# Loading the first tile as two halves on two queues, and half of the key weights on a third, at the head of a two-layer linear-attention and MLP kernel

## The chip, the cores and the metric

The kernel runs on one core of a Trainium2 chip. The metric is the device time of one execution in microseconds (us). Before the change it is 323.23 us, the median of three runs (323.01 to 323.62).

The engines are named as the profile names them: PE (TensorE, matrix multiplications; PEld its weight loads), DVE (VectorE), ACT (ScalarE), POOL (GpSimd) and SP (SyncE, which here only issues DMAs). A letter q behind an engine's name (SPq, ACTq, POOLq) means its instruction queue, for instance when it issues a DMA.

## What is computed

x has 2048 tokens of 512 features in bf16. Two blocks, A and B, are applied in turn, twice over, each with a residual:

```python
def _A_ref(x, wqkv, wo):            # linear attention, 32 heads of 16
    q, k, v = heads of (x @ wqkv)
    phi = lambda t: jnp.where(t > 0, t + 1, jnp.exp(t)) + 1e-6
    pq, pk = phi(q), phi(k)
    kv = jnp.einsum("bhsd,bhse->bhde", pk, v)
    z = jnp.einsum("bhsd->bhd", pk)
    o = einsum(pq, kv) / (einsum(pq, z)[..., None] + 1e-6)
    return merged(o) @ wo

def _B_ref(x, w1, b1, w2, b2):      # MLP, 512 -> 1792 -> 512
    y = _layernorm(x, axis=-1)
    h = _gelu(jnp.einsum("bsd,df->bsf", y, w1) + b1)
    return jnp.einsum("bsf,fd->bsd", h, w2) + b2

x = x + _A_ref(_layernorm(x), A_wqkv, A_wo)
x = x + _B_ref(_layernorm(x), B_w1, B_b1, B_w2, B_b2)
x = x + _A_ref(_layernorm(x), A_wqkv, A_wo)
x = x + _B_ref(_layernorm(x), B_w1, B_b1, B_w2, B_b2)
```

## The kernel before

**Tiling.** The tokens are 16 tiles of 128 (numbered 0 to 15), in four chunks of four tiles: chunk c is rows 512c to 512c+511, and partition p of it holds four neighbouring rows, one for each tile. Everything stays in on-chip memory between the blocks; the inputs are read once and the result is written once.

**An order written out by hand.** The kernel first builds a graph of named operations (`G.op`), each with its engine, what it reads and what it writes. `CONF["ORDER"]` lists for every engine the names in the order in which they are issued, and `CONF["PLACES"]` says which buffer slot each tile takes. `Settled.run` (line 144) takes both as they stand; nothing is chosen while the program runs. An engine waits at an instruction until everything that this one reads is there, and all that is listed behind it on that engine waits too. `assign_waits` (line 186) turns the dependencies into semaphore waits.

**The loads at the start.** `CONF["LOADS"]` (line 243) lists them: name, issuing queue, what, and behind which earlier operation. SP issues `x0` (tile 0, 128 KB), `x1` (tiles 1 to 3, 384 KB), `wka` and `wkc` (quarters 0 and 1 of the key weights, 128 KB each), then `xc1` (chunk 1, 512 KB), which waits until `x0` has landed, then `wq` (512 KB, query weights), `xc3`, and, behind the first two DMA transposes, `xc2`. ACT issues `wkb` (quarter 2), held until the constant `onesm` is written, and `wkd` (quarter 3). A quarter d is rows 128d to 128d+127 of the 512x512 key weights, the contraction slice of one matmul.

**The head, tile by tile.** While the loads are under way PE runs warm-up matmuls on a constant (`warm0`, seven of 512 columns, and `warm1` to `warm8`, of 256). For tile 0, DVE makes statistics (`statsA0_0`, line 775; `aggrA0_0`, line 777) and centres the tile (`cenA0_0`, line 789); PE transposes it (`PTC0`, line 825, four transposes); ACT copies the transposed tile out (`tcC0`, line 835). Then PE multiplies it with the four quarters of the key weights, in four separate operations `K0_0a` to `K0_0d` in the order that `ks0` gives ("2|0|3|1"). The division by the standard deviation, a power on POOL (`vepsA0_0`, line 782, `powA0_0`, line 784), follows as a scale on ACT (`expk0_0`, line 847, `reluk0_0`, line 858); DVE ends phi with `mink0_0` (line 860) and `phik0_0` (line 864). Tile 1 goes the same way (`cenA0_1`, `PTC1`, `tcC1`, `K0_1`, which needs all four quarters). Tiles 2 and 3 are normalised on DVE (`normA0_2`, `normA0_3`, line 803) before PE transposes them (`PTA0_2`, `PTA0_3`, copies `tcA0_2`, `tcA0_3`). The statistics of tile 3 are made on ACT (`sumA0_3`, line 766, stands ahead of `tcC0` in ACT's order). On DVE `statsA0_5`, which needs chunk 1, stands ahead of `normA0_3`. From tile 4 on the transposes are DMAs on SP (`TA0_n`, line 812).

With the key features `pk` of a tile, PE adds to the running product of normalised input and keys (`G0_n_0`, line 984). Query projections (`Q0_c_k`, lines 896 and 909) stand in between; the first, `Q0_0_*`, needs the transposes of all four tiles of chunk 0 and `wq`.

**POOL's order** starts with the small constants `id0`, `neghalf`, `bdm0`, `bdm1`, `id1` (lines 719 to 734: the identity for PE's transposes and the block-diagonal mask), and goes on with `vepsA0_0`, `powA0_0`, `negA0_3` and so on. Its own DMAs (`wv`, `wo`, `w1`, `w2`, line 728) come some 30 us later.

After the head come the attention's output (line 1123), the MLP (lines 1153 and 1190), and the second layer in the same manner.

Of the kernel before, what the change touches and what calls it, by code (L numbers as in the profile page):

```python
# [1359 lines left out]
```

## Time and profile before

| | |
|---|---|
| median of the runs | 323.23 us (323.01 to 323.62) |
| the profiled execution | 323.1 us, of which the profile's span is 321.9 us |
| PE busy in the span | 318.0 us (99%) |
| DVE, ACT, POOL busy | 218.1, 189.3, 145.5 us (68%, 59%, 45%) |
| read from and written to memory | 8.00 and 2.10 MB |
| granted TensorE clock, mean | 1.00 |

In the views of the profile a row of the timeline is: start in us from the span's start, duration in us, engine, line of the kernel, operation, what is written and read, number of instructions merged in the row, and, in brackets, the idle time of the engine ahead of it with what ended it. A row of the DMA view is: destination, source, issuing queue, number of DMAs, size of each, and the median time in us from issue to landing. Consecutive matmuls overlap in the pipeline: four of 512 columns in a row show 1.03 us, and the next four start 0.86 us after them.

### The profile page before, as it was taken

To read this page: it belongs to the slowest core of one execution; us is meant where nothing else is said; L and a number is where in the kernel's file an instruction comes from. 1 tells how busy PE (TensorE), PEld (TensorE's weight loads), DVE (VectorE), ACT (ScalarE), POOL (GpSimd) and SP (SyncE) were. 2 spreads that over 40 slices of the span, in tenths; PEclk is the share of its full clock that TensorE was granted. 3 is DMA by queue.
4 is the path that set the end of the run, shared out by engine and by line. 5 is a ranking of instruction groups with operands and counts; after the bars stand their busy time and mean duration, and the time that the engine had idled before them with its cause. 6 is when DMAs were issued, how large, how long until landed. Compare 5 with 4: busy or idle time off the path is not lost.

```text
span 321.9 us, 4748 instructions
## 1 busy us (share of the span) xinstructions
PE 318.0 (99%) x1703; PEld 157.4 (49%) x1703; DVE 218.1 (68%) x529; ACT 189.3 (59%) x324; POOL 145.5 (45%) x216
## 2 busy tenths in 40 slices
PE   8999999999999999999999999999999999999997
PEld 3444554666444444444444444558544444444444
DVE  5998789999786774028848899999889881101103
ACT  5898656797730636667962367979634442663320
POOL 6573978688655355101822415887454163000000
...
DMA packets 52355, 21.68 MB, mean 67 GB/s; under 512 B 47532, under 2 KB 50860, under 8 KB 52332
## 3 DMA queue, kind: packets, MB, share of 16 engines
...
q10 hardware_dynamic: 432, 0.30, 0.3%
q8 instruction: 13, 0.21, 0.3%
q14 instruction: 10, 0.08, 0.1%
HBM read 8.00 MB, written 2.10 MB: 31 GB/s over the span
## 4 chain that ended last, share of the span: by engine, by line
PE 97%; DMA 2%; DVE 0%; issue 0%
PE ps L1153 30%; PE ps L1190 29%; PE ps L1123 9%; PE ps L879 8%; PE ps L896 6%; PE ps L984 4%; PE ps L1013 4%; DMA t<-in_A_x_dram 2%; PE ps L909 2%; PE ps L1176 1%; PE ps L970 1%; PE ps L1034 1%; PE ps L1057 1%; PE ps L1100 1%; DVE stats L775 0%; PE ps L1048 0%
## 5 line engine op out<-in xcount | busy, mean ns | idle before, releaser
L1158 ACT ACTIVATE gT<-ps,b1c 128x512 bf16<-128x512 f32 (+1 forms) x140 | 77.0, 601 | 68.7 <-PE ps L1153 68.1
L1153 PE MATMUL ps<-t,w 128*128 128x512 bf16 (+1 forms) x560 | 102.5, 336 | 0.0
L1190 PE MATMUL ps<-w,gT 128*128 128x512 bf16 x434 | 98.6, 379 | 0.0
L1153 PEld LDWEIGHTS ps<-t,w 128*128 128x128 bf16 x560 | 54.8, 98 | 43.7 <-ACT gT L1158 0.2
L1190 PEld LDWEIGHTS ps<-w,gT 128*128 128x128 bf16 x434 | 42.5, 98 | 50.4
L784 POOL TENSOR_TENSOR rstd<-veps,neghalf 128x1 f32<-128x1 f32 x64 | 39.0, 625 | 41.1 <-DVE veps L782 38.9
L847 ACT ACTIVATE eb<-ps 128x512 bf16<-128x512 f32 x62 | 35.4, 606 | 19.3 <-PE ps L896 7.3
L1200 DVE TENSOR_TENSOR yb<-ps,xsb 128x512 bf16<-128x512 f32 x15 | 10.2, 688 | 41.4 <-PE ps L1190 41.4
L775 DVE BATCH_NORM_STATS2 stats<-xsb 128x6 f32<-128x512 f32 x48 | 32.0, 681 | 0.3
L1123 PE MATMUL ps<-gtb,t 128*128 128x512 bf16 x128 | 31.4, 379 | 0.0
L879 PE MATMUL ps<-wqkv,t 128*128 128x512 bf16 x128 | 30.9, 379 | 0.3 <-ACT t L835 0.3
L858 ACT ACTIVATE rb<-ps 128x512 bf16<-128x512 f32 x43 | 25.3, 607 | 5.8 <-PE ps L879 5.8
L798 ACT ACTIVATE yb<-xsb,nmr,rstd 128x512 bf16<-128x512 f32 x21 | 16.9, 814 | 15.1 <-POOL nmr L795 15.1
L896 PE MATMUL ps<-wqkv,t 128*128 128x512 bf16 x96 | 24.1, 379 | 0.0
L1089 POOL TENSOR_TENSOR t<-t,rr 128x512 bf16<-128x512 bf16 x18 | 19.3, 1072 | 9.0 <-DVE rr L1085 6.4
L782 POOL TENSOR_SCALAR veps<-mv 128x1 f32<-128x1 f32 x35 | 8.2, 236 | 32.7 <-DVE mv L777 31.3
L1196 DVE TENSOR_TENSOR xsb<-ps,xsb 128x512 f32<-128x512 f32 x16 | 10.8, 678 | 17.9 <-PE ps L1190 17.9
L1139 POOL TENSOR_TENSOR xsb<-xsb,b2b 128x512 f32<-128x512 f32 x17 | 21.4, 1267 | 3.0 <-DVE yb L803 2.9
L1077 POOL TENSOR_TENSOR lr<-t,zrow 128x512 f32<-128x512 bf16 x14 | 16.5, 1179 | 7.3 <-ACT zrow L997 4.5
L1123 PEld LDWEIGHTS ps<-gtb,t 128*128 128x128 bf16 x128 | 12.5, 98 | 14.5
L803 DVE TENSOR_SCALAR yb<-xsb,mv,rstd 128x512 bf16<-128x512 f32 x27 | 14.5, 542 | 7.3 <-POOL rstd L784 6.0
L879 PEld LDWEIGHTS ps<-wqkv,t 128*128 128x128 bf16 x128 | 12.1, 98 | 14.7 <-ACT t L835 0.9
...
## 6 DMA issues: line engine op xcount, KB each, us to landing
...
out_dram<-yb SPq DMA_DIRECT2D x15, 128.0 KB, 2.0
t<-in_A_x_dram SPq DMA_DIRECT2D x3, 512.0 KB, 4.8
t<-yb SPq DMA_TRANSPOSE x62, 2.5
wqkv<-in_A_wqkv_dram SPq DMA_DIRECT2D x1, 512.0 KB, 5.9
wqkv<-in_A_wqkv_dram POOLq DMA_DIRECT2D x1, 512.0 KB, 4.7
wo<-in_A_wo_dram POOLq DMA_DIRECT2D x1, 512.0 KB, 5.3
t<-in_A_x_dram SPq DMA_DIRECT2D x1, 384.0 KB, 3.3
```

Source lines behind the costliest of these rows:

```text
L775: G.op("dve", lambda e: e.bn_stats(stats[:, s.slot, :], src()), 620, reads=src_keys, writes=[k + "s"], tiles=[s, *src_tiles], name=f"stats ...
L784: G.op("pool", lambda e: e.tensor_tensor(rstd[:, s.slot:s.slot + 1], veps[:, s.slot:s.slot + 1], neghalf[:], op=ALU.pow), 570, reads=[k + ...
L847: G.op("act", lambda e: e.activation(eb[:, et.slot, :], bank(bt), ACT.Exp, scale=by()), 478, reads=[src_key, *more_keys], writes=[f"e{tag} ...
L858: G.op("act", lambda e: e.activation(rb[:, rt.slot, :], bank(bt), ACT.Relu, scale=by()), 478, reads=[src_key, *more_keys], writes=[f"r{tag ...
L879: ins = e.matmul(bank(b), lhsT=yTa(yT)[:, dt, k * P:(k + 1) * P], rhs=wqkv[:, dt, D:2 * D], start=(i == 0 and n == 0), stop=(i == len(part ...
L896: ins = e.matmul(bank(b), lhsT=yTa(yT)[:, dt, k * P:(k + 1) * P], rhs=wqkv[:, dt, 0:D], start=(dt == 0), stop=(dt == DT - 1))
L1089: lambda e, d=d, tok=tok, heads=heads: e.tensor_tensor(heads(tok()), heads(tok()), rr[:, d.slot, :].unsqueeze(2).broadcast_to([P, H, DH]), ...
L1123: ins = e.matmul(bank(wb), lhsT=yTa(pq)[:, kt, k * P:(k + 1) * P], rhs=gtb[:, kt, :], start=(kt == 0), stop=(kt == DT - 1))
L1139: G.op("pool" if on_pool else "dve", lambda e: e.tensor_tensor(xsb[:, st, :], xsb[:, st, :], b2b[:], op=ALU.add), 1120 if on_pool else 600 ...
L1153: ins = e.matmul(bank(b, n), lhsT=w1[:, dt, ft * P:(ft + 1) * P], rhs=yTa(yT)[:, dt, k0 * P:k1 * P], start=(dt == 0), stop=(dt == DT - 1))
L1158: G.op("act", lambda e, ft=ft, b=b, k0=k0, k1=k1, n=n: e.activation(gT[:, g.slot, ft * 512 + k0 * P:ft * 512 + k1 * P], bank(b, n), ACT.Ge ...
L1190: ins = e.matmul(bank(b), lhsT=gT[:, g.slot, ft * 512 + k * P:ft * 512 + (k + 1) * P], rhs=w2[:, ft, :], start=(ft == 0), stop=(ft == FT - 1))
```

## The change

1. `x0` is cut in two DMAs of 64 partitions each: `x0a` first on SP's queue, `x0b` first on ACT's. `xc1` now waits for both.
2. Of the key weights, quarter 0 (`wkb`) is issued by ACT behind `x0b`, without the hold on `onesm`; quarter 1 (`wka`) by SP in the place of before; quarters 2 and 3 (`wkp`, one DMA of 256 KB) by POOL, behind `id1` and ahead of `vepsA0_0`. `wkc` and `wkd` are gone.
3. `ks0` becomes "0|1|23": `K0_0c` now holds the two matmuls of quarters 2 and 3, and `K0_0d` is gone.
4. The orders of all engines are listed anew for the head, up to about the first MLP matmuls; from there on they are the same name by name. `PLACES` changes with them. Two of the tiny operations `veps` move from DVE to POOL (`vepsA0_12`, `vepsB0_7`).
5. New code that this configuration does not use: chunk orders (`CHUNKS` is 0, 1, 2, 3 in all three stages, the order of before) and a mixed form of the denominator (`by_half`, which no chunk asks for).

```diff
-    LOADS=[['x0', 'sp', 'x', 0, 0, 1, ''], ['x1', 'sp', 'x', 0, 1, 4, ''],
-           ['wkb', 'act', 'wk', 0, 2, 3, 'ones'], ['wka', 'sp', 'wk', 0, 0, 1, ''],
-           ['wkd', 'act', 'wk', 0, 3, 4, ''], ['wkc', 'sp', 'wk', 0, 1, 2, ''],
-           ['xc1', 'sp', 'x', 1, 0, 4, 'x0'], ['wq', 'sp', 'wq', 0, 0, 4, ''], ...
+    LOADS=[['x0a', 'sp', 'half', 0, 0, 0, ''], ['x0b', 'act', 'half', 1, 0, 0, ''],
+           ['x1', 'sp', 'x', 0, 1, 4, ''], ['wkb', 'act', 'wk', 0, 0, 1, ''],
+           ['wka', 'sp', 'wk', 0, 1, 2, ''], ['wkp', 'pool', 'wk', 0, 2, 4, ''],
+           ['xc1', 'sp', 'x', 1, 0, 4, 'x0a x0b'], ['wq', 'sp', 'wq', 0, 0, 4, ''], ...
...
 "sp":
-  "x0 x1 wka wkc xc1 wq xc3 TA0_0 TA0_1 xc2 TA0_5 TA0_4 TA0_7 ...
+  "x0a x1 wka xc1 wq xc3 TA0_0 TA0_1 TA0_5 TA0_4 xc2 TA0_7 ...
 "pe":
-  "warm0 warm8 warm2 warm6 PTC0 warm1 warm7 warm5 warm4 warm3 K0_0a K0_0b PTC1 K0_0c K0_0d
-   PTA0_2 K0_1 PTA0_3 K0_2 K0_3 G0_0_0 G0_1_0 Q0_0_2 Q0_0_1 Q0_0_0 K0_5 G0_2_0 K0_4 ...
+  "warm0 warm7 warm4 warm5 warm8 PTC0 warm1 warm6 warm3 warm2 K0_0a K0_0b PTC1 K0_0c
+   PTA0_2 K0_1 PTA0_3 K0_2 G0_0_0 K0_3 G0_1_0 Q0_0_1 Q0_0_2 Q0_0_0 K0_5 G0_2_0 K0_4 ...
 "act":
-  "wkb wkd sumA0_3 tcC0 sqA0_3 tcC1 reluk0_0 tcA0_2 expk0_0 tcA0_3 expk0_1 reluk0_1 ...
+  "x0b wkb sumA0_3 tcC0 sqA0_3 tcC1 expk0_0 tcA0_2 reluk0_0 expk0_1 tcA0_3 reluk0_1 ...
 "dve":
-  "... normA0_2 statsA0_5 normA0_3 aggrA0_5 normA0_1 statsA0_4 mink0_0 aggrA0_4 phik0_0 ...
+  "... normA0_2 statsA0_5 normA0_3 normA0_1 mink0_0 aggrA0_5 phik0_0 statsA0_4 mink0_1 ...
 "pool":
-  "id0 neghalf bdm0 bdm1 id1 vepsA0_0 powA0_0 negA0_3 vepsA0_2 ...
+  "neghalf id0 bdm0 bdm1 id1 wkp vepsA0_0 powA0_0 negA0_3 vepsA0_2 ...
...
-        "ks0": "2|0|3|1"
+        "ks0": "0|1|23"
...
+        def load_half(name, queue, h, after):
+            G.parts[("x0", 0)] = (("x0", 0, 0), ("x0", 0, 1))
+            ps_ = slice(64 * h, 64 * h + 64)
+            loaded[name] = dma(queue, lambda e: e.dma_start(
+                t4[ps_, x0[0].slot, 0:D].rearrange("p (k d) -> p k d", k=1), rows(x_dram, 0)[ps_, 0:1, :]),
+                [("x0", 0, h)], [x0[0]], name=name, kb=64, after=after)
```

More of the change, by code (lines that the diff above doesn't have):

```diff
@@ L242 @@
     WARM=[[512, 512, 512, 512, 512, 512, 512], [256], [256], [256], [256], [256], [256], [256], [256]],
-    LOADS=[['x0', 'sp', 'x', 0, 0, 1, ''], ['x1', 'sp', 'x', 0, 1, 4, ''], ['wkb', 'act', 'wk', 0, 2, 3, 'ones'], ['wka', 'sp', 'wk', 0, 0, 1, ''], ['wkd', 'act', 'wk', 0, 3, 4, ''], ['wkc', 'sp', 'wk', 0, 1, 2, ''], ['xc1', 'sp', 'x', 1, 0, 4, 'x0'], ['wq', 'sp', 'wq', 0, 0, 4, ''], ['xc3', 'sp', 'x', 3, 0, 4, ''], ['xc2', 'sp', 'x', 2, 0, 4, '']],
+    LOADS=[['x0a', 'sp', 'half', 0, 0, 0, ''], ['x0b', 'act', 'half', 1, 0, 0, ''], ['x1', 'sp', 'x', 0, 1, 4, ''], ['wkb', 'act', 'wk', 0, 0, 1, ''], ['wka', 'sp', 'wk', 0, 1, 2, ''], ['wkp', 'pool', 'wk', 0, 2, 4, ''], ['xc1', 'sp', 'x', 1, 0, 4, 'x0a x0b'], ['wq', 'sp', 'wq', 0, 0, 4, ''], ['xc3', 'sp', 'x', 3, 0, 4, ''], ['xc2', 'sp', 'x', 2, 0, 4, '']],
+    CHUNKS=[[0, 1, 2, 3], [0, 1, 2, 3], [0, 1, 2, 3]],
     ORDER={
         "sp":
[1 row of a table removed]
[1 row of a table added]
             "TA0_11 b1 Tb1 TP0_1_3 b2 TP0_1_1 TP0_1_0 TP0_1_2 TB0_0 TB0_1 TB0_2 TB0_3 TB0_7 TP0_2_1 TB0_5 TB0_4 TB0_6 TP0_2_2 "
@@ L709, in load_w @@
                                [f"{which}_{d}" for d in range(d0, d1)], name=name, kb=128 * (d1 - d0), after=after)
+        def load_half(name, queue, h, after):
[4 more added lines that the diff above has]
+                [("x0", 0, h)], [x0[0]], name=name, kb=64, after=after)
         for name, queue, what, at, lo, hi, behind in cf["LOADS"]:
             after = [loaded[b] for b in behind.split()]
-            if what == "x":
+            if what == "half":
+                load_half(name, queue, at, after)
+            elif what == "x":
                 load_x(name, queue, at, lo, hi, after)
@@ L751, in build_kernel, with by_token, by_half @@
             G.op("pe", warm, sum(cols) / 1.2, tiles=[wu], name=f"warm{n}", n=len(cols))
-        def by_token(L, c):
-            return eng(f"den{L}_{c}") == "tok"
+        def by_token(L, c, k=0):
+            way = eng(f"den{L}_{c}")
+            return way == "tok" or (way == "half" and k >= 2)
+        def by_half(L, c):
+            return eng(f"den{L}_{c}") == "half"
+        tokq = {}
         def norm(src, src_keys, src_tiles, double, on_act, tag, src16=False, head=False, centred=None):
@@ L887, in attn_q, with fn @@
         def attn_q(L, c, yT, pq):
-            if by_token(L, c):
-                for k in range(4):
+            half = by_half(L, c)
+            own = pq
+            if half:
+                own = tokq[(L, c)] = Tile(T4, f"pqt{L}_{c}")
+            n = 2 * P if half else 4 * P
+            if not by_token(L, c):
+                for kt in range(DT):
+                    b = Tile(psum, f"q{L}_{c}_{kt}" + "c" * half, "q")
+                    def fn(e, kt=kt, b=b):
+                        for dt in range(DT):
+                            ins = e.matmul(bank(b, n), lhsT=wqkv[:, dt, kt * P:(kt + 1) * P], rhs=yTa(yT)[:, dt, 0:n],
+                                           start=(dt == 0), stop=(dt == DT - 1))
+                        return ins
+                    G.op("pe", fn, 4 * MM if n == D else 4 * (n / 2.4 + 2.5), reads=[f"yT{L}_{4 * c + k}" for k in range(n // P)] + ["wq"], writes=[f"q{L}_{c}_{kt}" + "c" * half],
+                         tiles=[b, yT], name=f"Q{L}_{c}_{kt}" + "c" * half, lat=MM_DRAIN, n=4)
+                    phi(b, f"q{L}_{c}_{kt}" + "c" * half, lambda kt=kt: yTa(pq)[:, kt, 0:n], f"pq{L}_{c}_{kt}" + "c" * half, [pq], f"q{L}_{c}_{kt}" + "c" * half, n=n)
+            for k in range(4):
+                if by_token(L, c, k):
                     b = Tile(psum, f"q{L}_{c}_{k}", "q")
@@ L900, in attn_q, with attn_z @@
                          tiles=[b, yT], name=f"Q{L}_{c}_{k}", lat=MM_DRAIN, n=4)
-                    phi(b, f"q{L}_{c}_{k}", lambda k=k: t4[:, pq.slot, k * D:(k + 1) * D], f"pq{L}_{c}_{k}", [pq],
+                    phi(b, f"q{L}_{c}_{k}", lambda k=k: t4[:, own.slot, k * D:(k + 1) * D], f"pq{L}_{c}_{k}", [own],
                         f"q{L}_{c}_{k}")
-                return
-            for kt in range(DT):
-                b = Tile(psum, f"q{L}_{c}_{kt}", "q")
-                def fn(e, kt=kt, b=b):
-                    for dt in range(DT):
-                        ins = e.matmul(bank(b), lhsT=wqkv[:, dt, kt * P:(kt + 1) * P], rhs=yTa(yT)[:, dt, :],
-                                       start=(dt == 0), stop=(dt == DT - 1))
-                    return ins
-                G.op("pe", fn, 4 * MM, reads=[f"yT{L}_{4 * c + k}" for k in range(4)] + ["wq"], writes=[f"q{L}_{c}_{kt}"],
-                     tiles=[b, yT], name=f"Q{L}_{c}_{kt}", lat=MM_DRAIN, n=4)
-                phi(b, f"q{L}_{c}_{kt}", lambda kt=kt: yTa(pq)[:, kt, :], f"pq{L}_{c}_{kt}", [pq], f"q{L}_{c}_{kt}")
         zfirst = {}
-        def attn_z(L, c, pks):
-            by_sum = [int(v) for v in (eng("zc0") or "").split()] if L == 0 else list(range(NC - 1))
+        def attn_z(L, c, pks, order):
+            by_sum = [int(v) for v in (eng("zc0") or "").split()] if L == 0 else order[:NC - 1]
+            others = [v for v in order if v not in by_sum]
             def fold(add):
@@ L973, in attn_z, with attn_g_held @@
             G.op("pe", fn, 400, reads=[f"pk{L}_{4 * c + k}" for k in range(4)] + ["onesm"], writes=[f"zc{L}_{c}"], tiles=[b, *pks], name=f"Z{L}_{c}", lat=MM_DRAIN, n=16)
-            total(b, f"zc{L}_{c}", f"zs{L}_{c}", bool(L) or c != min(v for v in range(NC) if v not in by_sum))
-            if L == 0 and by_sum and c == max(v for v in range(NC) if v not in by_sum):
+            total(b, f"zc{L}_{c}", f"zs{L}_{c}", bool(L) or c != others[0])
+            if L == 0 and by_sum and c == others[-1]:
                 fold(True)
-        def attn_g_held(L, st, k, y, ykey, pk, gb):
-            parts = [(dc,) for dc in range(DT)] if st == ST - 1 else [tuple(range(DT))]
+        def attn_g_held(L, st, k, y, ykey, pk, gb, first, last):
+            parts = [(dc,) for dc in range(DT)] if last else [tuple(range(DT))]
             for part in parts:
@@ L984, in fn @@
                         ins = e.matmul(ps[:, gb.slot + dc, :], lhsT=yb[:, y.slot, dc * P:(dc + 1) * P], rhs=pkb[:, pk.slot, :],
-                                       start=(st == 0), stop=(st == ST - 1))
+                                       start=first, stop=last)
                     return ins
                 keys = [f"g{L}_{dc}" for dc in part]
-                G.op("pe", fn, len(part) * MM, reads=[ykey, f"pk{L}_{st}"] + (keys if st else []), writes=keys,
+                G.op("pe", fn, len(part) * MM, reads=[ykey, f"pk{L}_{st}"] + ([] if first else keys), writes=keys,
                      tiles=[y, pk, gb], name=f"G{L}_{st}_{part[0]}", lat=MM_DRAIN, n=len(part))
@@ L1004, in attn_g_out, with attn_g_chunk @@
                 copy(gtb[:, dc, :], gb, f"g{L}_{dc}", ("gt", dc), dc % 2, f"g{L}_{dc}", off=dc)
-        def attn_g_chunk(L, c, ys, ykeys, pks):
+        def attn_g_chunk(L, c, ys, ykeys, pks, first, last):
             for dc in range(DT):
@@ L1017, in attn_g_chunk @@
                      tiles=[b, *ys, *pks], name=f"G{L}_{c}_{dc}", lat=MM_DRAIN, n=4)
-                if c == 0:
+                if first:
                     G.op("dve", lambda e, dc=dc, b=b: e.tensor_scalar(gacc[:, dc, :], bank(b), 1.0, None, op0=ALU.mult), 600,
                          reads=[f"g{L}_{c}_{dc}"], writes=[("gacc", dc)], tiles=[b], name=f"ga{L}_{c}_{dc}", lat=40)
-                elif c < NC - 1:
+                elif not last:
                     G.op("dve", lambda e, dc=dc, b=b: e.tensor_tensor(gacc[:, dc, :], bank(b), gacc[:, dc, :], op=ALU.add), 600,
@@ L1042, in attn_kv @@
                  reads=["zs", "bdmask"], writes=["zb"], name=f"zb{L}", lat=40, fast=True)
-            if any(by_token(L, c) for c in range(NC)):
+            if any(by_token(L, c, 3) for c in range(NC)):
                 zr = Tile(psum, f"zr{L}", "t")
@@ new lines, in attn_den @@
+            half = by_half(L, c)
+            src = tokq[(L, c)] if half else pq
+            pt = pq if half or not by_token(L, c) else Tile(T4, f"pt{L}_{c}")
+            n = 2 * P if half else 4 * P
+            if not by_token(L, c):
+                for kt in range(DT):
+                    tag = f"{L}_{c}_{kt}" + "c" * half
+                    b = Tile(psum, f"d{tag}", "n")
+                    r = Tile(LR, f"lr{tag}")
+                    key = f"pq{L}_{c}_{kt}" + "c" * half
+                    G.op("pe", lambda e, kt=kt, b=b: e.matmul(bank(b, n), lhsT=zb[:, kt * P:(kt + 1) * P], rhs=yTa(pq)[:, kt, 0:n], start=True, stop=True),
+                         MM if n == D else n / 2.4 + 2.5, reads=[key, "zb"], writes=[f"d{tag}"], tiles=[b, pq], name=f"D{tag}", lat=MM_DRAIN)
+                    G.op("act", lambda e, b=b, r=r: e.activation(lr[:, r.slot, 0:n], bank(b, n), ACT.Ln, bias=eps6[:]), 575 if n == D else 362,
+                         reads=[f"d{tag}", "eps6"], writes=[f"l{tag}"], tiles=[b, r], name=f"ln{tag}", lat=90, table="exp")
+                    G.op("act", lambda e, r=r: e.activation(lr[:, r.slot, 0:n], lr[:, r.slot, 0:n], ACT.Exp, scale=-1.0), 536 if n == D else 323,
+                         reads=[f"l{tag}"], writes=[f"l{tag}"], tiles=[r], name=f"rec{tag}", lat=110, table="exp")
@@ new lines, in attn_den, with tok, heads @@
+                         (1150 if on_pool else 600) if n == D else (580 if on_pool else 330),
+                         reads=[f"l{tag}", key], writes=[key], tiles=[r, pq], name=f"pr{tag}", lat=40,
+                         fast=not on_pool)
+            for k in range(4):
+                if not by_token(L, c, k):
+                    continue
+                tag = f"{L}_{c}_{k}"
+                r = Tile(LR, f"lr{tag}")
+                d = Tile(RD, f"rd{tag}")
+                def tok(k=k):
+                    return t4[:, src.slot, k * D:(k + 1) * D]
+                def heads(ap):
+                    return ap.rearrange("p (h x) -> p h x", x=DH)
+                on_pool = eng(f"pz{tag}") != "dve"
+                G.op("pool" if on_pool else "dve",
+                     lambda e, r=r, tok=tok: e.tensor_tensor(lr[:, r.slot, :], tok(), zrow[:], op=ALU.mult), 1150 if on_pool else 600,
+                     reads=[f"pq{tag}", "zrow"], writes=[f"l{tag}"], tiles=[r, src], name=f"pz{tag}", lat=60,
+                     fast=not on_pool)
+                G.op("dve", lambda e, r=r, d=d, heads=heads: e.tensor_reduce(rd[:, d.slot, :], heads(lr[:, r.slot, :]),
+                                                                              mybir.AxisListType.X, ALU.add), 600,
+                     reads=[f"l{tag}"], writes=[f"rd{tag}"], tiles=[r, d], name=f"red{tag}", lat=60)
+                G.op("dve", lambda e, d=d: e.tensor_scalar(rd[:, d.slot, :], rd[:, d.slot, :], 1e-6, None, op0=ALU.add), 100,
+                     reads=[f"rd{tag}"], writes=[f"rd{tag}"], tiles=[d], name=f"den{tag}", lat=60)
+                G.op("dve", lambda e, d=d: e.reciprocal(rr[:, d.slot, :], rd[:, d.slot, :]), 300,
+                     reads=[f"rd{tag}"], writes=[f"rr{tag}"], tiles=[d], name=f"rec{tag}", lat=60)
@@ new lines, in attn_den, with attn_out @@
+                     1150 if on_pool else 600, reads=[f"rr{tag}", f"pq{tag}"], writes=[f"pq{tag}"], tiles=[d, src],
+                     name=f"pr{tag}", lat=60, fast=not on_pool)
+                dma("sp", lambda e, k=k, tok=tok: e.dma_start_transpose(yTa(pt)[:, :, k * P:(k + 1) * P], tok()), [f"pt{tag}"],
+                    tiles=[src, pt], reads=[f"pq{tag}"], name=f"TP{tag}", sem=("pT", src, k), transpose=True)
+            return pt
+        def attn_out(L, c, k, pq, base, base_keys, base_tiles, first):
@@ L1116, in attn_out @@
             st = 4 * c + k
             wb = Tile(psum, f"wo{L}_{st}", "w")
-            parts = [(kt,) for kt in range(DT)] if st == 0 else [tuple(range(DT))]
+            parts = [(kt,) for kt in range(DT)] if first else [tuple(range(DT))]
             for part in parts:
@@ L1141, in mlp_front, with mlp_up @@
                  fast=not on_pool)
[L1143 to L1145 removed]
+        def mlp_up(L, c, yT, g, first):
+            parts = [(0, 2), (2, 4)] if first else [(0, 4)]
             for hf, (k0, k1) in enumerate(parts):
@@ L1206, in build_kernel @@
         gb = Tile(psum, "g4", "g4", 4)
-        pq1, trs = [], []
-        for c in range(NC):
+        pq1, trs = {}, []
+        orders = cf["CHUNKS"]
+        for c in orders[0]:
             yT = Tile(T4, f"yT0_{c}")
             pq = Tile(T4, f"pq0_{c}")
-            pq1.append(pq)
+            pq1[c] = pq
             pks = []
@@ L1252, in build_kernel @@
         for L in range(2):
-            nxt = []
-            for c in range(NC):
+            nxt = {}
+            chunks = orders[1 + L]
+            for c in chunks:
                 yT = Tile(T4, f"yBT{L}_{c}")
```

87 lines of the change are left out of this document (22 added, 65 removed), and 293 rows, old and new, of tables (ORDER, PLACES, WAY).

## The prediction

> **What bounds the kernel now.** I read the page first, then PE in four stretches, then the chain that ended last, then PE's own timeline at the head.
>
> ```profile
> span 321.9 us, 4748 instructions
> ```
> ```profile
> 0.00:9.39 9.39, 7.50 (x39) 3.16 (x40) 5.67 (x16) 5.43 (x10) 5.69 (x18) 1.00 0.78 277
> 9.39:12.85 3.46, 3.46 (x20) 1.44 (x18) 3.36 (x12) 3.26 (x7) 1.80 (x4) 1.00 0.80 127
> 12.85:318.00 305.15, 305.15 (x1629) 151.44 (x1628) 208.19 (x502) 180.59 (x309) 138.01 (x195) 1.00 0.25 60
> ```
> ```profile
> 0.79 2.44 DMA t<-in_A_x_dram
> 3.24 4.83 DMA t<-in_A_x_dram
> ```
>
> The first figure behind a stretch's length is PE's busy time. From 9.39 us on PE never pauses: 3.46 of 3.46 us and 305.15 of 305.15 us. So the time can change only by what happens ahead of that, plus a new pause behind it. The chain names the two transfers that set the head: `x0` (issued 0.79, landed 3.23), and `xc1`, issued when `x0` is there, landed 8.07.
>
> ```profile
> 4.61 0.40 PE L825 MATMUL ps<-idp,yb 128*128 128x128 bf16 x4 [0.15 <-DVE yb L789]
> 4.84 0.72 PE L749 MATMUL ps<-const-bfloat16-1.0 128*128 128x256 bf16 x5
> 5.86 0.60 PE L879 MATMUL ps<-wqkv,t 128*128 128x512 bf16 x2 [0.30 <-ACT t L835]
> 6.55 0.40 PE L825 MATMUL ps<-idp,yb 128*128 128x128 bf16 x4
> 6.78 0.59 PE L879 MATMUL ps<-wqkv,t 128*128 128x512 bf16 x2
> 7.43 0.40 PE L825 MATMUL ps<-idp,yb 128*128 128x128 bf16 x4
> 7.67 1.03 PE L879 MATMUL ps<-wqkv,t 128*128 128x512 bf16 x4
> 9.16 0.40 PE L825 MATMUL ps<-idp,yb 128*128 128x128 bf16 x4 [0.47 <-DVE yb L803]
> 9.39 1.89 PE L879 MATMUL ps<-wqkv,t 128*128 128x512 bf16 x8
> 11.12 1.89 PE L984 MATMUL ps<-pkb,yb 128*128 128x512 bf16 x8
> 12.85 2.75 PE L909 MATMUL ps<-t,wqkv 128*128 128x512 bf16 x12
> ```
>
> In order: `PTC0`, warm-ups, `K0_0a` and `K0_0b`, `PTC1`, `K0_0c` and `K0_0d`, `PTA0_2`, `K0_1`, `PTA0_3`, `K0_2` and `K0_3`, `G0_0` and `G0_1`, and at 12.85 `Q0_0`. Up to `Q0_0` the changed kernel does the same PE work in nearly the same order, and behind it PE has no pause. I therefore use the start of `Q0_0` as the mark: **the time moves by as much as the mark moves from 12.85.**
>
> The steps cost, on PE: four transposes 0.24 (7.43 to 7.67), four matmuls of 512 columns 0.86 (11.12 to 12.85 is eight), so two 0.43.
>
> **The change part by part.** *Half of the key weights by POOL (`wkp`).* This is the term that matters, because `K0_0c` now needs quarters 2 and 3, both in `wkp`, and on PE everything is queued behind `K0_0c`. When is it issued? POOL does it behind `id1`:
>
> ```profile
> 3.25 0.29 POOL L720 TENSOR_SCALAR_AFFINE_SELECT idp<-idp 128x128 bf16<-128x128 bf16 x1
> 4.25 0.34 POOL L782 TENSOR_SCALAR veps<-mv 128x1 f32<-128x1 f32 x1 [0.71 <-DVE mv L777]
> 4.68 0.56 POOL L784 TENSOR_TENSOR rstd<-veps,neghalf 128x1 f32<-128x1 f32 x1
> ```
>
> `id1` ends at 3.54, so the issue starts at about 3.57, more than 1.4 us later than any quarter was issued before (the last one landed at 6.10, and the SP pair below takes 4.0 in the median: about 2.1). The only like transfer here is `wv`, also the first DMA of POOL, the same rows, but 512 KB and on quiet DMA engines:
>
> ```profile
> 32.54 0.97 POOL L728 DMA_DIRECT2D wqkv<-in_A_wqkv_dram  x1
> ```
> ```profile
> wqkv<-in_A_wqkv_dram POOLq DMA_DIRECT2D x1, 512.0 KB, 4.7
> ```
> ```profile
> q0 software_dynamic: 149, 0.54, 99.1%
> ```
> ```profile
> wqkv<-in_A_wqkv_dram SPq DMA_DIRECT2D x1, 512.0 KB, 5.9
> t<-in_A_x_dram SPq DMA_DIRECT2D x1, 384.0 KB, 3.3
> wqkv<-in_A_wqkv_dram ACTq DMA_DIRECT2D x2, 128.0 KB, 3.8
> wqkv<-in_A_wqkv_dram SPq DMA_DIRECT2D x2, 128.0 KB, 4.0
> t<-in_A_x_dram SPq DMA_DIRECT2D x1, 128.0 KB, 2.4
> ```
> ```profile
> 7.00:8.00 1.00, 0.95 (x8) 0.43 (x7) 0.38 (x1) 1.00 (x2) 0.91 (x3) 1.00 1.05 369
> ```
>
> The queue row is from 35.2 to 36.6 us: 0.54 MB in 1.4 us, so 256 KB less saves 0.68 us of `wv`'s 4.7: 4.0 on quiet engines. But at the head they are not quiet: from 7 to 8 us the DMA share is 1.05, `xc1` and `wq` being under way. What does load cost? The quarters took 3.8 and 4.0 us under load where `x0`, of the same size, took 2.4 ahead of it: 1.4 to 1.6. `xc1` took 4.8 where `wv`, as large, took 4.7: 0.1. Between 0.1 and 1.6 I take 0.5, nearer to the low end, as `wkp` competes mostly with `xc1` and with nothing ahead of it in its own queue. So `wkp` takes 4.5 us and **lands at T = 8.1**. Both ends: 2.4 us, the quickest load at the head (T = 6.0), and 5.9, that of `wq` (T = 9.5).
>
> [...]
>
> *From T to the mark.* ACT's and DVE's steps:
>
> ```profile
> 4.60 0.63 ACT L766 ACTIVATE eb<-t 128x512 bf16<-128x512 bf16 x1 [2.52 <-DMA t<-in_A_x_dram]
> 5.13 0.19 ACT L766 ACTIVATION_READ_ACCUMULATOR eb<-t 128x1 f32 x1
> 5.23 0.58 ACT L835 ACTIVATE t<-ps 128x512 bf16<-128x512 bf16 x1
> ```
> ```profile
> 10.09 0.68 ACT L847 ACTIVATE eb<-ps,rstd 128x512 bf16<-128x512 f32 x1
> 10.66 0.69 ACT L858 ACTIVATE rb<-ps,rstd 128x512 bf16<-128x512 f32 x1
> ```
> ```profile
> 10.32 0.43 DVE L864 TENSOR_TENSOR pkb<-eb,rb 128x512 bf16<-128x512 bf16 x1
> ```
>
> The copy ends at 5.81 and PE starts at 5.86, so a hand-over to PE costs about 0.06. `K0_0c` starts at T+0.06, issues 0.43 and is visible after 0.59 (row 6.78): T+0.65. In the new order ACT has `expk0_0` ahead of the copy `tcA0_2`: exponential from T+0.69, next instruction 0.57 later (10.09 to 10.66), copy from T+1.26 to T+1.85, `K0_2` at T+1.91. PE's own work would allow T+1.83 (0.06+0.43+0.24+0.86+0.24), so ACT decides by 0.1. `K0_2` lasts to T+2.77; the new order has `G0_0` next, which needs `reluk0_0` (0.48 behind the copy's start, 0.69 long, T+2.43) and then `phik0_0` (0.43, T+2.90): `G0_0` at T+2.96, `K0_3`, `G0_1` and `Q0_0` 0.86 apart: **the mark at T+5.54**. It equals 12.85 at T = 7.31. With T = 8.1 it is 13.64, **0.8 us later**.
>
> *What hides behind that.* `xc1`: of what stood ahead of it in the hardware queues 256 KB are gone, 0.68 us by the same rate, so about 7.4 in place of 8.07, if it is issued as early. That frees DVE, whose order keeps `statsA0_5` (8.09) ahead of `normA0_3` (8.70), and so `PTA0_3`:
>
> ```profile
> 6.41 0.41 DVE L803 TENSOR_SCALAR yb<-t,mv,rstd 128x512 bf16<-128x512 bf16 x1
> 6.73 0.14 DVE L782 TENSOR_SCALAR veps<-mv 128x1 f32<-128x1 f32 x1
> 6.96 0.41 DVE L803 TENSOR_SCALAR yb<-t,mv,rstd 128x512 bf16<-128x512 bf16 x1
> 8.09 0.69 DVE L775 BATCH_NORM_STATS2 stats<-t 128x6 f32<-128x512 bf16 x1 [0.72 <-DMA t<-in_A_x_dram]
> 8.70 0.40 DVE L803 TENSOR_SCALAR yb<-t,stats,rstd 128x512 bf16<-128x512 bf16 x1
> ```
>
> That gain of up to 0.63 us (`K0_1` ends its issue at 8.53, `PTA0_3` starts at 9.16) is real but lies under `wkp`: at T = 8.1 `PTA0_3` cannot start before T+1.59 = 9.69 on PE's side.
>
> *The halves.* Cost and gain on the path: nothing. `x0` landing earlier would start `PTC0` earlier, but the new order puts one more warm-up ahead of it (0.83+3.63 = 4.46 for ten, and 0.11 to 0.21 for one more), so 4.6 stays; and its copy waits for `sumA0_3`, which `x1` (landed 4.58) lets start at 4.60, so `K0_0a` stays at 5.86. If this cover goes because `x1` comes earlier as well, the gain is at most as large as `x1`'s; if `x0b` is late, see the second rival.
>
> *POOL behind `wkp`.* Its issue takes 0.97, to 4.54, so `vepsA0_0` is 0.3 late and the power ends at 5.5 in place of 5.24; its first reader is at 6.41. Hidden. *SP*: one issue fewer, `wka` and `xc1` as early as before; the move of `xc2` behind `TA0_4` brings `TA0_5` forward, which a later mark does not need. *The other orders* I cost at nothing, between -0.2 and +0.3: the engines beside PE have 97 us (DVE, 305.15-208.19) and more of slack in the long stretch, but in its first 3.46 us DVE is busy 3.36.
>
> **Sum.** 323.1 (profiled execution: span 321.9 and 1.2 around it) + 0.8 = **323.9 us**, against the median of 323.23 shown 0.2% slower.
>
> **Rivals.** *1, not slower: `wkp` is early enough and hidden.* From T = 7.3 down the mark moves ahead one for one, until `K0_0c` is at its old 6.78 (T = 6.7); then `PTA0_3` follows `K0_1` at 8.53 and the gain is its 0.63, less about 0.1 for `G0_0` waiting for `phik0_0`: 322.6. With `x1` also 0.3 earlier, 322.3. [...] Against it: `wv`'s 4.7 us, which leaves 7.6 even without any load. Chance 0.26.
>
> *2, `x0b` is late on ACT's queue.* ACT's loads took 3.8 us where SP's `x0` took 2.4. If `x0b` takes 3.8, it lands at 4.6 and holds `xc1`, with `wq` and `xc3` queued behind it on SP: `xc1` at 7.4+1.4 = 8.8, and as `PTA0_3` comes 1.09 behind it (8.07 to 9.16), the mark moves by 0.7: 323.8. It decides only if T is under 8.0. Against it: ACT's quarters were issued behind `x1` and into busy engines. Chance 0.12.
>
> *3, the halves reach the end by themselves,* 0.2 us of `x0` carried to the mark: 322.9; this needs the two covers above gone. [...] Chance 0.04.
>
> **How the numbers follow.** The forecast, `wkp` decides, has 0.58; with T between 7.3 and 9.0 it covers 323.1 to 324.8. About 0.2% (0.65 us, that is 322.58 and 323.88) is what a measurement of this kernel tells from no change. Slower by more: T over 7.95, 0.44 of the forecast's 0.58, and most of rival 2, 0.08: 0.52. Faster by more: rival 1 with `x1` early, 0.16. Same: 0.32. The range of 8 in 10 reaches from 322.5 (rival 1) to 324.8 (T = 9.0).
>
> **What would show it.** Right: in PE's timeline the first matmul of the key projection behind the second four transposes has an idle time ahead of it of about a microsecond, ended by a DMA into `wqkv`; POOL's issue at 3.6 and its landing near 8; `Q0_0`'s first row near 13.6 and no PE idle behind it. Wrong: `wkp` landing under 7.3; `PTA0_3` again waiting for DVE (rival 2); or a pause of PE after 14 us, which would blame the orders.

## The result and the profile after

The changed kernel takes 326.62 us (median, 325.58 to 326.96) against 323.42 before: the ratio is 1.0097 (1.0074 to 1.0119). The forecast was 323.9, with 324.8 as the range's upper end. Timed again beside other runs (last experiments), the same kernel is at 324.57, ratio 1.0049 (1.0023 to 1.0076). It is slower in both, by an amount that itself varies. Why it varies belongs to the answer.

The page's first line, and PE in the stretches of the head, the third one now ending where `Q0_0` starts:

```profile
span 325.6 us, 4722 instructions
```
```profile
0.00:9.39 9.39, 5.42 (x25) 2.24 (x25) 5.61 (x15) 3.90 (x7) 6.45 (x18) 1.00 0.76 254
9.39:12.85 3.46, 3.07 (x16) 1.61 (x17) 1.02 (x4) 2.41 (x5) 0.74 (x2) 0.68 0.83 143
12.85:16.66 3.81, 3.76 (x15) 1.58 (x15) 3.52 (x12) 2.84 (x7) 1.02 (x4) 0.84 0.17 34
```

PE is busy 5.42 us up to 9.39, where it was 7.50 before. The third figure from the right is new: the granted clock of PE, 1.00 throughout before, is 0.68 in the second stretch and 0.84 in the third. The start of PE's chain of waits (start, length, what) says what released it:

```profile
2.46 0.85 POOL bdmask L743
3.30 0.20 POOL idp L729
3.50 6.23 DMA wqkv<-in_A_wqkv_dram
9.73 0.05 issue
9.78 0.60 PE ps L894 x2
```

Before, the chain went through `x0` and `xc1`. Now it is POOL's constants (`bdmask`, the block-diagonal mask, and `idp`, the identity) and then `wkp`, issued at 3.50 and landed 6.23 us later, at 9.73. PE's timeline:

```profile
4.99 0.40 PE L840 MATMUL ps<-idp,yb 128*128 128x128 bf16 x4 [0.58 <-DVE yb L804]
...
6.07 0.61 PE L894 MATMUL ps<-wqkv,t 128*128 128x512 bf16 x2 [0.24 <-ACT t L850]
6.79 0.40 PE L840 MATMUL ps<-idp,yb 128*128 128x128 bf16 x4
9.78 0.60 PE L894 MATMUL ps<-wqkv,t 128*128 128x512 bf16 x2 [2.60 <-DMA wqkv<-in_A_wqkv_dram]
10.22 0.39 PE L840 MATMUL ps<-idp,yb 128*128 128x128 bf16 x4
10.45 1.71 PE L894 MATMUL ps<-wqkv,t 128*128 128x512 bf16 x4
11.95 0.63 PE L840 MATMUL ps<-idp,yb 128*128 128x128 bf16 x4
12.38 1.86 PE L894 MATMUL ps<-wqkv,t 128*128 128x512 bf16 x4
14.07 1.03 PE L1004 MATMUL ps<-pkb,yb 128*128 128x512 bf16 x4
14.94 1.03 PE L894 MATMUL ps<-wqkv,t 128*128 128x512 bf16 x3
15.80 1.03 PE L1004 MATMUL ps<-pkb,yb 128*128 128x512 bf16 x4
16.66 2.75 PE L915 MATMUL ps<-t,wqkv 128*128 128x512 bf16 x12
```

`K0_0c`, behind the second group of four transposes, waits 2.60 us for `wkp`. Behind it, four matmuls of 512 columns (`K0_1`) take 1.71 us, where they take 1.03 at 14.07. The mark, the start of `Q0_0`, is at 16.66 instead of 12.85, 3.81 later. The span is 3.7 longer, so all of the loss lies ahead of the mark. The clock in finer stretches (the clock is again the third figure from the right):

```profile
10.20:10.60 0.40, 0.40 (x6) 0.32 (x5) 0.00 (x0) 0.18 (x1) 0.00 (x0) 1.00 2.89 175
10.60:14.00 3.40, 3.40 (x13) 1.49 (x11) 1.93 (x6) 3.33 (x6) 0.74 (x2) 0.51 0.23 47
14.00:14.40 0.40, 0.40 (x3) 0.20 (x2) 0.35 (x2) 0.12 (x1) 0.00 (x0) 0.93 0.00 0
```

It is 0.51 for 3.4 us, and the fall comes some 0.8 us after PE has started again. So the loss seems to have two parts: the late load, and a clock that fell after the wait. The experiments test both.

### The profile page after: what moved, and what is told of

It is laid out like the page before. It is cut to its first block, busy times and chain, and to the rows that moved or that the text cites. A ratio compares the mean times of both kernels' runs of the same rounds, so it can differ in the third digit from the quotient of the medians.

```text
span 325.6 us, 4722 instructions
## 1 busy us (share of the span) xinstructions
PE 317.7 (98%) x1673; PEld 158.2 (49%) x1703; DVE 217.8 (67%) x527; ACT 188.9 (58%) x324; POOL 145.2 (45%) x219
## 3 DMA queue, kind: packets, MB, share of 16 engines
q0 software_dynamic: 1136, 4.98, 4.5%
## 4 chain that ended last, share of the span: by engine, by line
PE 96%; DMA 2%; issue 1%; POOL 1%; DVE 0%
PE ps L1178 30%; PE ps L1215 29%; PE ps L894 9%; PE ps L1148 8%; PE ps L927 6%; PE ps L1033 4%; PE ps L1004 4%; PE ps L915 2%; DMA wqkv<-in_A_wqkv_dram 2%; PE ps L1201 1%; PE ps L1054 1%; PE ps L990 1%; PE ps L1077 1%; PE ps L1093 0%; POOL bdmask L740 0%
## 5 line engine op out<-in xcount | busy, mean ns | idle before, releaser
L799 POOL TENSOR_TENSOR rstd<-veps,neghalf 128x1 f32<-128x1 f32 x64 | 37.7, 605 | 40.7 <-DVE veps L797 38.9
L894 PE MATMUL ps<-wqkv,t 128*128 128x512 bf16 x125 | 32.3, 393 | 3.1 <-DMA wqkv<-in_A_wqkv_dram 2.6
L927 PE MATMUL ps<-wqkv,t 128*128 128x512 bf16 x94 | 23.6, 379 | 0.1
L875 DVE TENSOR_SCALAR eb<-eb 128x512 bf16<-128x512 bf16 x45 | 14.2, 320 | 7.9 <-ACT eb L862 7.9
```

Of the source, the lines that this page charges most:

```text
L799: G.op("pool", lambda e: e.tensor_tensor(rstd[:, s.slot:s.slot + 1], veps[:, s.slot:s.slot + 1], neghalf[:], op=ALU.pow), 570, reads=[k + ...
L894: ins = e.matmul(bank(b), lhsT=yTa(yT)[:, dt, k * P:(k + 1) * P], rhs=wqkv[:, dt, D:2 * D], start=(i == 0 and n == 0), stop=(i == len(part ...
L927: ins = e.matmul(bank(b), lhsT=yTa(yT)[:, dt, k * P:(k + 1) * P], rhs=wqkv[:, dt, 0:D], start=(dt == 0), stop=(dt == DT - 1))
```

## The experiments

"T" is when `wkp` lands and "the mark" the start of `Q0_0`, as in the prediction.

**Only the load on POOL's queue undone.** The halves and the new orders stay.

```diff
-['wkp', 'pool', 'wk', 0, 2, 4, '']
+['wkd', 'act', 'wk', 0, 3, 4, ''], ['wkc', 'sp', 'wk', 0, 2, 3, '']
```

> The changed kernel with only the load on POOL's queue undone: quarter 3 of the key weights goes on ACT's queue and quarter 2 on SP's, where loads of that kind stood before; the halves of x0 and all new orders stay. Theory L (the load on POOL's queue lands at 9.73 us, and with the clock that falls behind the wait it is the whole loss): the quarters land by about 6.1, the 2.60 us wait of PE on line 894 is gone, PE's clock stays at 1.00, the first query projection starts at 12.3 to 12.9, and the time is 322.6 to 323.4 us. Rival O (the halves or the new orders cost the time, the load only shows where PE happens to wait): over 325 us, with another wait in its place.

323.17 us (ratio 0.9997, 0.9984 to 1.0010). PE's timeline:

```profile
7.01 0.59 PE L894 MATMUL ps<-wqkv,t 128*128 128x512 bf16 x2
...
12.89 2.75 PE L915 MATMUL ps<-t,wqkv 128*128 128x512 bf16 x12
```

No wait ahead of `K0_0c`, and the mark is at 12.89 (12.85 before). The halves and the new orders together are worth nothing that can be measured. Theory L holds and rival O falls.

**Only the load on POOL's queue, in the kernel before.**

```diff
-['wkb', 'act', 'wk', 0, 2, 3, 'ones'], ... ['wkd', 'act', 'wk', 0, 3, 4, ''], ['wkc', 'sp', 'wk', 0, 1, 2, '']
+['wkb', 'act', 'wk', 0, 1, 2, 'ones'], ... ['wkp', 'pool', 'wk', 0, 2, 4, '']
-"ks0": "2|0|3|1"
+"ks0": "0|1|23"
```

> The kernel before with only the load on POOL's queue: quarters 2 and 3 in one DMA behind the identity, the keys of tile 0 in the parts 0, 1 and 2 with 3; x0 is whole and all other orders are those of before. Theory L: the load lands 5.5 to 6.5 us after its issue, 9.1 to 10.0, PE waits 2 us or more for it at the third part, the clock falls to 0.5 for some 3 us, and the time is 325.5 to 327. Rival O (halves and orders): 323.2 to 323.6, as before. In between (324 to 325) the parts share it.

327.46 us (ratio 1.0128, 1.0107 to 1.0149), even above theory L's range (325.5 to 327), as `wkp` took 6.89 us. From its chain, then from PE's timeline:

```profile
3.50 6.89 DMA wqkv<-in_A_wqkv_dram
```
```profile
10.43 0.89 PE L879 MATMUL ps<-wqkv,t 128*128 128x512 bf16 x2 [3.65 <-DMA wqkv<-in_A_wqkv_dram]
...
17.31 1.03 PE L909 MATMUL ps<-t,wqkv 128*128 128x512 bf16 x4
```

One edit makes the whole loss. T is 10.39 and the mark is T+6.92; in the changed kernel it is T+6.93 (16.66-9.73). The forecast had T+5.54.

**PE kept busy while the load is under way.** The added warm-ups compute nothing that is used.

```diff
-    WARM=[..., [256], [256]],
+    WARM=[..., [256], [256], [512] * 14],
-... warm3 warm2 K0_0a
+... warm3 warm2 warm9 K0_0a
```

> The changed kernel with 14 more warm-up matmuls of 512 columns (3.0 us) ahead of the first part of tile 0's keys, so that PE is busy while the load on POOL's queue is under way; the part that needs the load starts at the same time, about 9.8. Theory C (the wait costs twice: once itself, and once because PE's clock falls to 0.50 behind an idle stretch): the clock stays at 1.00, the first query projection starts at about 15.3 in place of 16.66, and the time is 1.1 to 1.5 us under the changed kernel's, 325.1 to 325.5. Rival D (the low clock between 10.6 and 14 us has another cause, or hides under the waits for ACT and DVE): the same 326.0 to 327.0.

```profile
wqkv<-in_A_wqkv_dram POOLq DMA_DIRECT2D x1, 256.0 KB, 6.3
```
```profile
9.49 0.39 PE L840 MATMUL ps<-idp,yb 128*128 128x128 bf16 x4
9.86 0.60 PE L894 MATMUL ps<-wqkv,t 128*128 128x512 bf16 x2
...
15.37 2.75 PE L915 MATMUL ps<-t,wqkv 128*128 128x512 bf16 x12
```

The clock is 1.00 in all stretches, and with T at 9.81 the mark is at 15.37: T+5.56, as theory C has it. The time did not follow as far: 326.03 us (325.12 to 326.63), 0.6 under the changed kernel where 1.1 to 1.5 was expected, and inside rival D's range. PE has one pause behind the mark, ahead of `K0_7`. Its row, and from the chain the transpose that it waited for:

```profile
22.98 1.02 PE L894 MATMUL ps<-wqkv,t 128*128 128x512 bf16 x4 [0.54 <-DMA t<-yb]
```
```profile
18.86 3.98 DMA t<-yb
```

It is the DMA transpose of tile 7 (`TA0_7`, of chunk 1), which SP issues right behind `xc2`. It took 3.98 us, where it took 2.4 in the changed kernel. `xc2`, in the DMA engines at the same time, took 4.98 and landed at 22.24. So 0.54 of the 1.29 us by which the mark is earlier is lost there.

**`wkp` issued 2 us earlier.**

```diff
-"neghalf id0 bdm0 bdm1 id1 wkp vepsA0_0 ...
+"neghalf id0 id1 wkp bdm0 bdm1 vepsA0_0 ...
```

> The changed kernel with the load on POOL's queue and the identity's second instruction ahead of the two instructions for the block mask, so that it is issued about 2 us earlier, at 1.3 to 1.5. Theory F (the queue has a fixed 6.2 us): it lands at 7.5 to 7.7, PE waits half a microsecond, and the time is 323.0 to 323.6. Theory Q (most of the 6.2 us is the other loads in the DMA engines at 6 to 9 us): it lands at 5.5 to 6.5, PE doesn't wait for it, and x1 or the quarters on the hardware queues land later for it by up to 0.7; 322.5 to 323.3. Rival O: over 325.

```profile
wqkv<-in_A_wqkv_dram POOLq DMA_DIRECT2D x1, 256.0 KB, 4.5
```
```profile
6.99 0.59 PE L894 MATMUL ps<-wqkv,t 128*128 128x512 bf16 x2
...
12.62 2.75 PE L915 MATMUL ps<-t,wqkv 128*128 128x512 bf16 x12
```

Issued at 1.45, it takes 4.54 us, lands at 5.99, and no wait is left. The price is small: `wka` lands at 6.25 instead of 5.35. 323.03 us (ratio 0.9991, 0.9981 to 1.0002). The 6.2 us are not the queue's own: theory Q.

**What lengthens the load: all later loads held behind it, or only some.** First `xc1` with `wq` and `xc3` behind it on SP's queue, then `wq` with `xc3` alone. A third run halves the bytes (quarter 2 by SP, as in the first experiment).

```diff
-['xc1', 'sp', 'x', 1, 0, 4, 'x0a x0b']
+['xc1', 'sp', 'x', 1, 0, 4, 'x0a x0b wkp']
...
-['wq', 'sp', 'wq', 0, 0, 4, '']
+['wq', 'sp', 'wq', 0, 0, 4, 'wkp']
...
-['wkp', 'pool', 'wk', 0, 2, 4, '']
+['wkp', 'pool', 'wk', 0, 3, 4, ''], ['wkc', 'sp', 'wk', 0, 2, 3, '']
```

> The changed kernel with chunk 1 (and on the same queue behind it the query weights and chunk 3) held back until the load on POOL's queue has landed; it's a measurement of that landing, as chunk 1 is then late by itself. Theory F (6.2 us are the queue's own): it lands at 9.5 to 9.9 as in the changed kernel. Theory Q (the other loads in the DMA engines between 6 and 9 us lengthen it): first packets 2 to 2.7 us behind the issue instead of 3.3, landing at 7.0 to 8.0. Either way the mark is late, at 15 to 17, and the time 325 to 328.

> The changed kernel with the query weights (and chunk 3 behind them on SP's queue) held until the load on POOL's queue has landed; chunk 1 stays where it is, issued at 3.6. It tells which of the later loads lengthens the one on POOL's queue. If chunk 1 (512 KB in the same engines at the same time) does most of it: landing at 8.5 to 9.7, and the time 324.8 to 326.5. If the query weights and chunk 3 do (they queue up behind chunk 1, so that the last completions of POOL's load wait for them): landing at 7.0 to 8.3, a wait of PE under 1.2 us, the clock at 1.00, the mark at the landing + 5.55, and the time 322.8 to 324.1.

> The changed kernel with only quarter 3 (128 KB) on POOL's queue and quarter 2 on SP's. If bytes set the landing (rate theory, 256 KB in some 1.6 us of packets) it comes 0.7 us earlier or more, at about 9.0 or under; if the way to the first packet (3.3 us) and the last completions behind the other loads do, it stays at 9.3 to 9.9 and the time at 325.5 to 327.

Each of the three was executed once. The landing in them, by the row of DMA issues (last figure: us from issue to landing) and twice by the chain:

```profile
wqkv<-in_A_wqkv_dram POOLq DMA_DIRECT2D x1, 256.0 KB, 3.4
```
```profile
3.50 4.21 DMA wqkv<-in_A_wqkv_dram
```
```profile
3.50 4.40 DMA wqkv<-in_A_wqkv_dram
```

The same DMA, issued at the same 3.50, takes 3.35 us with nothing behind it, 4.21 with `xc1` beside it, and 6.23 with all three. So in these executions `xc1` costs 0.86, and `wq` and `xc3` another 2.0. As the load with all three takes 4.96 to 7.81 (last section), the second figure can be anything from 0.8 to 3.6. With 128 KB it takes 4.40 although all three are there, 1.8 less than 6.23 and 0.6 less than the shortest of the full loads; 0.7 or more was expected if the bytes set the landing. The packets of POOL's queue (number, MB, share of the DMA engines), first from 5 to 6 us with all later loads held back:

```profile
q0 software_dynamic: 35, 0.14, 80.2%
```

And in the changed kernel, from 6 to 7, 7 to 8, 8 to 9, and 9 to 9.75 us:

```profile
q0 software_dynamic: 6, 0.02, 6.0%
```
```profile
q0 software_dynamic: 64, 0.22, 61.2%
```
```profile
q0 software_dynamic: 8, 0.02, 14.6%
```
```profile
q0 software_dynamic: 2, 0.00, 0.1%
```

More than half of the lengthening stands at the start: the first packet comes at 6.80 in the changed kernel, at 6.17 with only `xc1` beside the load, and at 5.16 with nothing, so 1.6 of the 2.9 us pass before any of its data moves. The rest is a tail. Nearly all the data has moved by 8.0 (0.24 MB in 70 packets), but a last few packets come up to 1.4 us later, while the hardware queue, with `wq` in it, takes 88% of the DMA engines (from 8 to 9). With `wq` held the last ones come by 7.2. That a load which is smaller, or ends before `wq` gets going, has less of this tail agrees with that and with the 128 KB run (4.40 us), but is the author's estimate, not tested by itself.

The times: 325.12 us with `xc1` held, where PE waits 2.28 us later on, for tile 3, which follows chunk 1 on DVE, and its clock stays at 1.00:

```profile
11.22 0.40 PE L840 MATMUL ps<-idp,yb 128*128 128x128 bf16 x4 [2.28 <-DVE yb L818]
```

With `wq` held it is 324.25, just above the range that was expected (0.60 us of waiting at `K0_0c`, then 0.61 at `Q0_0` for a DMA transpose, which SP issues behind the held `wq` and which landed at 14.00; `wq` itself was there at 11.6), and with 128 KB 324.46. PE in the last:

```profile
7.95 0.60 PE L894 MATMUL ps<-wqkv,t 128*128 128x512 bf16 x2 [0.84 <-DMA wqkv<-in_A_wqkv_dram]
...
13.46 2.75 PE L915 MATMUL ps<-t,wqkv 128*128 128x512 bf16 x12
```

T is 7.90, the wait 0.84, the clock stays at 1.00, and the mark is T+5.56.

**Half the filling.** Seven added warm-ups instead of 14.

> The changed kernel with 7 instead of 14 more warm-up matmuls (1.5 us), so that PE's wait for the load is about 1.1 us in place of 2.6. If a short wait leaves the clock alone: clock 1.00 throughout, the mark at 15.3 to 15.5, and a lost microsecond costs a microsecond. If any wait of that order lowers it: 0.50 for some 3 us behind the wait, and the mark at 16.4 to 16.8.

The aim, a wait of 1.1 us, was missed: `wkp` took 7.81 us in this execution, so PE waited 3.32 after all and the clock fell. From the chain, from PE's timeline, and by stretches:

```profile
3.50 7.81 DMA wqkv<-in_A_wqkv_dram
```
```profile
11.36 0.61 PE L894 MATMUL ps<-wqkv,t 128*128 128x512 bf16 x2 [3.32 <-DMA wqkv<-in_A_wqkv_dram]
```
```profile
12.00:15.30 3.30, 3.30 (x15) 1.58 (x13) 1.90 (x6) 3.00 (x6) 0.74 (x2) 0.50 0.21 40
```

328.44 us (one execution), with T at 11.31 and the mark at 18.23: T+6.92 again. It does not tell how short a wait leaves the clock alone, but shows how far the landing spreads.

**`wkp` early and `x0` whole.** On top of the early issue, `x0` goes on SP's queue in one piece, as before the change. The holds of before come back with it: `wkb` behind `onesm`, `xc1` behind `x0`.

```diff
-['x0a', 'sp', 'half', 0, 0, 0, ''], ['x0b', 'act', 'half', 1, 0, 0, '']
+['x0', 'sp', 'x', 0, 0, 1, '']
```

> The run with the early load on POOL's queue, but x0 whole on SP's queue as in the kernel before. Theory H (the halves cost a little at the head: the second lands at 3.5 where the whole tile lands at 3.2, and the first transposes start at 4.96 in place of 4.6): PTC0 at about 4.6, K0_0a at 5.8, chunk 1 issued 0.4 us earlier and there by 7.3; the mark 12.2 to 12.5 and 322.3 to 322.8 us, 0.1 to 0.5 under that run. Rival N (the halves are hidden, DVE's normalisation of tile 3 sets the mark either way): 322.8 to 323.2, the same. Rival G (the halves help): over 323.3.

```profile
6.80 0.59 PE L894 MATMUL ps<-wqkv,t 128*128 128x512 bf16 x2
...
12.53 2.75 PE L915 MATMUL ps<-t,wqkv 128*128 128x512 bf16 x12
```

322.55 us (322.43 to 323.23), ratio 0.9983 (0.9969 to 0.9996): the only version here whose interval lies wholly below the kernel before. The mark is at 12.53, at the edge of what theory H expected. Beside the halved version (0.9991, 0.9981 to 1.0002) the intervals overlap, so what the halves cost by themselves at the end isn't settled.

**The same in the old orders.** Early `wkp`, whole `x0`, and the orders of the kernel before.

```diff
-"id0 neghalf bdm0 bdm1 id1 vepsA0_0 ...
+"id0 neghalf id1 wkp bdm0 bdm1 vepsA0_0 ...
```

> The orders of the kernel before, x0 whole, and the load on POOL's queue issued early (ahead of the block mask, at about 1.45): the run with the early load and the whole x0, but without the new orders. If the new orders are worth nothing by themselves: the mark at 12.4 to 12.7 and 322.3 to 322.9 us, as in that run. If they carry its gain over the kernel before: 323.0 to 323.4. If they cost: under 322.3.

323.06 us, ratio 0.9989 (0.9974 to 1.0005). The mark is earliest of all, 12.27, yet the span is 321.9 as before. What PE waited for after 13 us:

```profile
PE ps L1153 <- DMA t<-yb: 0.4, 1, 0.4
```

It is a transposed tile at the start of the MLP, between 60 and 70 us, where PE had no pause before. In this execution most of the 0.58 us gained at the head is given back there; the 128 KB run shows the same wait, of 0.6. In the new orders with early `wkp` no such wait was seen, in one profile each. By the expectation this time means that the new orders carry the gain of the run before. But the two intervals overlap (0.9974 to 1.0005 and 0.9969 to 0.9996), so that isn't settled.

**The changed kernel and the filled one again.** Both unaltered, side by side on one chip.

> The changed kernel as it is, timed again beside the filled one on the same chip, for the spread of its time and its mean clock run by run. Theory C (the wait also lowers the clock for 3.4 us, which costs 1.4): most runs 326 to 327.5 with a mean clock of 0.995; a run whose clock stays at 1.000 is more than 1 us faster, at 324.8 to 325.8.

> The kernel with 14 more warm-up matmuls in the wait, timed again in more rounds, as its four runs overlapped with the changed kernel's. Theory C: clock 1.000 in all runs and a median 0.8 to 1.4 us under the changed kernel's in this call. Rival D (the low clock hides under other waits, or what is won is lost again at chunk 2's late load): within 0.4 us of it.

The changed kernel: 324.57 us (324.04 to 328.03). Nine of twelve runs have a mean clock of 1.000 and take 324.04 to 325.02; the other three, with 0.990 and 0.995, take 326.47 to 328.03. In the first measurement three of four were at 0.995, and most runs were expected to be so here. One at 1.000:

```profile
3.50 4.96 DMA wqkv<-in_A_wqkv_dram
```
```profile
8.51 0.61 PE L894 MATMUL ps<-wqkv,t 128*128 128x512 bf16 x2 [1.20 <-DMA wqkv<-in_A_wqkv_dram]
...
14.02 2.75 PE L915 MATMUL ps<-t,wqkv 128*128 128x512 bf16 x12
```

T is 8.46, the wait 1.20, the clock 1.00, the mark T+5.56, the time 324.23. The filled kernel: clock 1.000 in all eight runs (and in the four of before), but 325.57 us (325.16 to 326.79), 1.0 slower than the changed one, which neither theory C nor rival D expected. In its profile the mark is T+5.55 (15.14-9.59), and then:

```profile
23.04 1.02 PE L894 MATMUL ps<-wqkv,t 128*128 128x512 bf16 x3 [0.83 <-DMA t<-yb]
```

So filling the wait keeps the clock but costs more than it saves where the clock would have held anyway. Part of the reason is the filling itself. The transposes ahead of `K0_0c` start at 9.49 and 9.16 in the two filled profiles and take 0.24, so `K0_0c` could not start before 9.73 or 9.40 however early `wkp` landed. In the changed kernel it starts at 8.51 when `wkp` lands at 8.46. That is 0.9 to 1.2 us, about the difference of the two times; no filled profile had such an early load, so this is argued.

## Why the prediction was wrong

**Right: where it happens.** The half on POOL's queue decides, `K0_0c` waits for it, and the time moves with the mark. The chain from T to the mark was T+5.54; at full clock it is T+5.55 or 5.56 in four profiles (T = 7.90, 8.46, 9.59, 9.81). Where `wkp` happened to land at 8.46, near the forecast's 8.1, the mark moved by 1.17 (12.85 to 14.02), which makes 324.27 of 323.1, and the profiled execution took 324.23.

**Wrong: the term "`wkp` takes 4.5 us".** It was built as 4.0 on quiet engines and 0.5 for load. Both are off, in opposite directions. Quiet it is 3.35, so the 0.68 taken off `wv`'s 4.7 was too little. The load costs 2.9 in the first profile (6.23-3.35), and 1.6 to 4.5 in all six with everything under way (4.96 to 7.81). The bounds 0.1 and 1.6 were taken from whole loads on the hardware queues; "nothing ahead of it in its own queue" was the reason for the low end, and it did not protect it: with the loads on SP's queue under way, its first packet came 1.6 us later and its last ones were spread out. What holds the packets up is not shown. T of 9.73 instead of 8.1 makes 1.63 us. The range was also cut at T = 9.0, below the working's own upper end of 9.5. And two starting points were mixed: "T over 7.95" counts from the median of 323.23, the sum from 323.1, by which 323.88 is reached at T = 8.09, so the chance of slower was set a little too high.

**Missing: a term for the clock.** The sum priced a microsecond of waiting at a microsecond, and put the clock at nothing without a word. The waits of 2.60, 3.32 and 3.65 us were each followed by about 3.4 us at a clock of 0.50 or 0.51, in the three profiles that had one, and the mark was T+6.92 or 6.93: 1.37 us more. This closes the sum: 13.64 + 1.63 + 1.39 = 16.66, the mark as measured. That it is the slow stretch which costs this is shown by the four profiles at full clock; in two of them, the filled ones, `wkp` landed as late as in the changed kernel.

What makes the clock fall is not shown. It fell behind a wait of 2.60, and not behind one of 2.28 (the run with `xc1` held). Where between these the bound lies, or whether something beside the length of the wait decides, no run here settles.

**The rivals.** The first (hidden, 322.6) did not occur as changed. With `wkp` issued early it occurs, at less than its figure with the halves (the mark 0.23 earlier, 323.03) and at it with `x0` whole (322.55). The second (`x0b` late) is refuted in size: `x0b` landed at 3.53, not 4.6, and `xc1` at 7.12. The third had no case: the first half landed at 3.23, just when the whole tile did, and the second 0.3 later.

```profile
3.63 0.69 DVE L790 BATCH_NORM_STATS2 stats<-t 128x6 f32<-128x512 bf16 x1 [2.18 <-DMA t<-in_A_x_dram]
```

DVE's first statistics start 0.4 later than before, and `PTC0` at 4.99 instead of 4.61. And `xc1`, "as early as before" in the prediction, was issued at 3.61 instead of 3.24, since it waits for the second half. So the step "cost on the path: nothing, 4.6 stays" was wrong locally and right at the end, since `wkp` covered it; with the quarters on the hardware queues, where nothing covers it, the mark is at 12.89.

**The new orders at nothing** held: 323.17 with everything but the load on POOL's queue. They lean on their own timing, though, as the waits for tile 7's transpose in the filled kernel show.
